# Sliding-window attention into a two-layer MLP on one core: weight slices in other places, and DMA transposes from step 13 on

## The chip, the core and the metric

One core of a Trainium2 chip runs the kernel. TensorE multiplies matrices into PSUM, VectorE, ScalarE and GpSimd work elementwise, and DMA queues move data between device memory and SBUF. Each engine takes its instructions in its own fixed order and waits at semaphores. SyncE computes nothing here: its queue issues nearly all DMAs, one after the other, and an entry that waits holds back all entries behind it. The metric is the device time of one execution in microseconds (us).

## The reference

Attention over 8 batches and 8 heads with 512 local and 32 global tokens each (head size 64), then a MLP over the 4608 rows of 512:

```python
def _attn_ref(q_l, k_l, v_l, q_g, k_g, v_g):
    ...
    s_g = scale * q_g @ k_all.T                  # 32 global queries see all 544 keys
    out_g = sm(s_g) @ v_all
    s_ll = where(abs(i - j) <= 32, scale * q_l @ k_l.T, -1e9)
    s_l = concatenate([scale * q_l @ k_g.T, s_ll])
    out_l = sm(s_l) @ concatenate([v_g, v_l])    # 512 local queries: window and globals
    return concatenate([out_g, out_l])

def _moe_ref(x, w_in, w_out):                    # 512 -> 2048 -> 512
    h = x @ w_in
    return (h / (1 + exp(-h))) @ w_out
```

All inputs and the output are float32.

## The kernel before

**Attention** is cut into 128 steps. A step k is one batch, one chunk of 128 queries and one pair of heads. Its parts are functions: `st_load` brings q and k into a `raw` tile (L314 for k < 28, L316 after), `st_split` makes two halves of them (k >= 28 only), `st_scores` does the scores s (L352 for k < 28) and the softmax (L359 to L368) into one of the `probs` tiles, `st_turn` transposes the probabilities on TensorE (L396) and copies them to a `pt` tile (L398), and `st_out` multiplies `pt` with v (o, L429) into the rows xh and xl of the MLP. From step KF = 24 on the transposes are done otherwise: `st_halves` has GpSimd sort the probabilities into two planes of 16 bit halves (L378, two copies a step), `st_away` writes these to device memory (L383), and `st_back` reads them back by a DMA transpose into `pt` (L387). Four `pt` tiles rotate. The 32 global queries go through `g_load` (L233), `g_scores` (L260), `g_soft` and `g_turn` (t and gt), four g steps a batch.

**The MLP** runs in 12 blocks n of 3 tiles (the last two: 2) of 128 rows. A block goes through the 16 slices f of the hidden layer: `first_layer` does 12 matmuls h (L584), then tanh on ScalarE (L590), gh and gl on VectorE and ScalarE (L591 to L594), and `second_layer` adds nine matmuls per f to the output banks (L606 to L608), one f later. The steps of the next block's tiles are spread over the matmuls of a block. Steps 0 to 13 come ahead of block 0, steps 14 to 25 lie in it.

**The weights** arrive as 64 bit words, only once, in slices i = 2f + half (half 0 the input weights of f, half 1 the output weights). `fetch_weights` issues the load of a slice (L195, names raw_w{i}), `join_weights` makes float32 of it on ScalarE (L213) and VectorE (L215, L216), and `split_weights` makes w_hi (ScalarE, L225) and w_lo (VectorE, L226), which h of that f waits for. In block 0, ahead of the first layer of f, the program joins up to f + 2 (LOOK) and fetches up to f + 5 (FETCH); the split of f + 1 follows.

**Places.** A slice's raw words lie in places that others use as well: half 0 of f in the place of w_hi of f; half 1 of f < 8 in that of w_hi of f + 8; half 1 of f >= 8 in the two `qk` tiles for odd f, and in the single tiles of the tags `o` and `halves` for even f. With two `qk` tiles, slice 27 (f = 13) has the place of slice 23 (f = 11). `raw_tile` gives a step's or a g step's load one of two `raws` tiles; for the first 28 steps and three batches of g loads it also uses the places 14 and 15 of later w_hi, four in rotation, until slices are fetched into these.

The order on TensorE and SyncE is written by the program: every part of a step has a due time, and the entries are emitted in the order of these times (`put`, `advance`, `fill`). On VectorE, ScalarE and GpSimd a scheduler sets the order.

Of the kernel before, what the change touches and what calls it, by code (L numbers as in the profile page):

```python
# [12 lines left out]
I32 = mybir.dt.int32  # L13
# [8 lines left out]
P = 128  # L22
# [5 lines left out]
SKV = SG + SL  # L28
DM, DFF = H * D, 2048
NCC, NF = DM // P, DFF // P  # L30
QW, KW, VW = 2 * P, 2 * W, 4 * D
# [5 lines left out]


SIZES = (3,) * 10 + (2, 2)
BUFS = dict(qk=2, raw=2, p=2, halves=1, pt=4)  # L40
ND = 28
KF = 24
GF = 3
KP = 12
WARM = 288
WARMS = (14, 8, 3)
SINGLE = 12
SCRATCH = 8
FETCH, LOOK = 6, 3
FIRSTW = {4: 2, 5: 2, 6: 1, 7: 1, 8: 1, 9: 1, 10: 1, 11: 1}  # L50
JOINS, SPLITS = (9.0, 9.6, 10.2, 10.8, 11.4, 12.0), (12.1, 12.7)

# [5 lines left out]
DMAT = dict(load=-1.65, halves=0.7, away=1.05, turn=1.3, back=1.65, out=2.7)  # L58
# [9 lines left out]
def attention_moe_kernel(ctx: ExitStack, tc: tile.TileContext, qk0_in, qk_in, v_in, gqk, wts, out):  # L68
    nc = tc.nc

    const = ctx.enter_context(tc.tile_pool(name="const", bufs=1))
    raws = ctx.enter_context(tc.tile_pool(name="raws", bufs=BUFS["raw"]))
    work = ctx.enter_context(tc.tile_pool(name="work", bufs=1))
# [23 lines left out]
    hold = tc.keep_in_program_order  # L97
    zeros = two.tile([P, WARM], BF16, tag="gl", bufs=1, name="zeros")
    nc.vector.memset(zeros, 0.0)

    def warm(bank, n):
        for _ in range(n):
            nc.tensor.matmul(bank[:, 512 - WARM :], zeros[:, :P], zeros, start=True, stop=True)

# [5 lines left out]

    probs = [const.tile([P, 2, 2 * P], F32, name=f"probs{i}") for i in range(BUFS["p"])]
    more = scratch(6, F32, "probs_")
# [9 lines left out]
    for kind in range(3):  # L122
# [7 lines left out]
        if kind == 0:  # L130
            hold(nc.gpsimd.memset(m[:, :HALO], NEG))
            pads()
            id32 = work.tile([P, P], F32R, tag="qk", bufs=BUFS["qk"], name="id32").bitcast(F32)
            make_identity(nc, id32)
# [9 lines left out]

    pts = [const.tile([P, 2, 2, P + SG], F32, name=f"pt{i}") for i in range(BUFS["pt"])]
    for t in pts:
# [5 lines left out]
    def probs_tile(k):  # L152
        i = k % (len(probs) if k < KP else BUFS["p"])
        held_by[i] = k
        return probs[i]
# [8 lines left out]
    def raw_tile(name, whole=False):  # L164
        i = next(homes) if whole else 0
        if whole and i == NPR:
            return scratch(13, F32, name)
        i = (i - (i > NPR)) % 4
        if i % 2 and 14 + i // 2 not in taken:
            return scratch(14 + i // 2, F32, name)  # L170
        return raws.tile([P, QW + KW], F32, tag="raw", name=name)

    def qk_tiles(name):
        return (work.tile([P, QW + KW], F32R, tag="qk", bufs=BUFS["qk"], name=f"qk{name}"),
                work.tile([P, SKV], F32R, tag="klo", bufs=BUFS["qk"], name=f"klo{name}"))

    w_32, w_hi, w_lo, w_raw, w_next = [], [], [], [], [0, 0]

    def fetch_weights():
        i = w_next[0]
        w_next[0] += 1
        f, half = divmod(i, 2)
        if half and f >= SCRATCH:
            homes_ = [work.tile([P, QW + KW], I32, tag="qk", bufs=BUFS["qk"], name=f"raw_w{i}_{q}")[:, :DM] if f % 2
                      else work.tile([P, DM], I32, tag="halves" if q else "o", bufs=1, name=f"raw_w{i}_{q}")
                      for q in range(2)]
        else:
            taken.add(f + SCRATCH * half)  # L190
            homes_ = [scratch(f + SCRATCH * half, I32, f"raw_w{i}")]
        n = DM // len(homes_)
        w_raw.append([(raw, q * n, n) for q, raw in enumerate(homes_)])
        for raw, c0, n in w_raw[i]:
            hold(nc.sync.dma_start(out=raw, in_=wts[f, :, DM * half + c0 : DM * half + c0 + n].bitcast(I32)))  # L195

    def join_weights():
        i = w_next[1]
        w_next[1] += 1
        while w_next[0] <= i:  # L200
            fetch_weights()
        f = i // 2
        if f + 1 == NF:
            w_32.append(work.tile([P, SKV], F32, tag="klo", bufs=BUFS["qk"], name=f"w{i}")[:, :DM])
        elif i % 2 == 0:
            w = const.tile([P, 2 * DM], F32, tag=f"ws{f + 1}", name=f"w{f}")
            w_32.extend((w[:, :DM], w[:, DM:]))
        for raw, c0, n in w_raw[i]:
            join_words(w_32[i][:, c0 : c0 + n], raw)
# [19 lines left out]
    state = {}  # L229

    def g_load(b, p):
        raw = raw_tile(f"raw_g{b}_{p}", b < GF)
        hold(nc.sync.dma_start(out=raw[:, :GW], in_=gqk[b, p]))  # L233
        state["graw", p] = raw

# [73 lines left out]
    tiles = {}  # L309

    def st_load(k, b, c, pr):
        raw = raw_tile(f"raw{k}", k < ND)
        if k < ND:
            hold(nc.sync.dma_start(out=raw[:, : QW + W], in_=qk0_in[k]))  # L314
        else:
            hold(nc.sync.dma_start(out=raw, in_=qk_in[k - ND]))  # L316
        tiles["raw", k] = raw
# [72 lines left out]
    def st_turn(k, b, c, pr):  # L390
        if k < KF:
            t = attbank("t", f"t{k}")
# [89 lines left out]
    at = 0.0  # L482

    def put(when, fn, *a):
        stream.append((when, fn, a))

    AHEAD = NPR
    for k, (t, b, c, pr) in enumerate(steps):
        a = (k, b, c, pr)
        j = k % NST  # L490
        due = dict(DUE)
        if k >= KF:
            due.update(DMAT if k >= ND else {part: DMAT[part] for part in DMAT if part != "load"})
            due.update({} if pr else DMAT0)
        if k < AHEAD:
            due.update({part: FIRST[part][k] - k for part in ("load", "vload", "turn", "out")})
        elif pr == 0:
            due["vload"] = VLOADS[min(k // NPR, 3)]
        if k == AHEAD:
            for h in range(NPR):  # L500
                put(FIRST["gload"][h], g_load, 0, h)
                put(FIRST["gscores"][h], g_scores, 0, h)
            for hh in range(2):
                put(FIRST["gsoft"][hh], g_soft, 0, hh)
                put(FIRST["gturn"][hh], g_turn, 0, hh)
            put(FIRST["late"], g_late)
            at = FIRST["then"]
            for when in JOINS:
                put(at + when - NPR, join_weights)
            for f, when in enumerate(SPLITS):  # L510
                put(at + when - NPR, split_weights, f)
        if j == 0 and b:
            for hh in range(2):
                put(at + (TURN if b > 1 else TURN1)[hh], g_turn, b, hh)
        for i in range(FIRSTW.get(k, 0)):
            put(at + 0.01, fetch_weights)
        put(at + due["load"], st_load, *a)
        put(at + due["split"], st_split, *a)
        put(at, st_scores, *a)
        if "vload" in due:  # L520
            put(at + due["vload"], st_vload, *a)
        if k >= KF:
            put(at + due["halves"], st_halves, *a)
            put(at + due["away"], st_away, *a)
        put(at + due["turn"], st_turn, *a)
        if k >= KF:
            put(at + due["back"], st_back, *a)
        if k < SINGLE or pr == NPR - 1:
            n = 1 if k < SINGLE else NPR
            put(at + due["out"], st_out, k - n + 1, n, b, c, t)  # L530
            marks[t] = at + due["out"]
        if j == NST - 1 and b % 4 == 3:
            put(marks[t] + 0.001, g_tile, t + 1)
            marks[t + 1] = marks[t] + 0.001
        if b + 1 < B:
            for h in [h for h in range(NPR) if int((HEADS if b else HEADS0)[0] + h * (HEADS if b else HEADS0)[1]) == j]:
                for part, fn in (("load", g_load), ("split", g_split), ("scores", g_scores)):
                    put(at + HEAD[part], fn, b + 1, h)
                if h % 2:
                    put(at + HEAD["soft"], g_soft, b + 1, h // 2)  # L540
                at += HEAD["slot"]
        at += 1.0
# [80 lines left out]
    for n in range(len(SIZES)):  # L623
        for f in range(NF):
            if n == 0:
                while w_next[1] < 2 * min(NF, f + LOOK):
                    join_weights()
                while w_next[0] < 2 * min(NF, f + FETCH):
                    fetch_weights()
            elif f == 0:  # L630
                advance(ends[n])
                now[:] = n, 0
            while len(w_hi) < NF and len(w_hi) <= NF * n + f + 1:
                split_weights(len(w_hi))
            g = first_layer(n, f)
            fill(SIZES[n])
            if pend is not None:
                second_layer(*pend)
            pend = (n, f, *g)
# [70 lines left out]
```

## Time and profile before

| | |
|---|---|
| median of 3 timed runs | 1020.4 us (1020.23 to 1022.18) |
| the profiled execution's own time | 1019.24 us |
| its span, first to last instruction | 1017.4 us |
| TensorE busy | 973.6 us, 96% |
| VectorE, ScalarE, GpSimd busy | 619.3, 580.6, 180.6 us |
| mean granted TensorE clock | 0.985 of full speed |
| DMA | 151.03 MB, 148 GB/s on the mean |

A busy share is a mean over stages with different limits: the attention ahead of block 0 (0 to 47 us), block 0, in which the weights come in, and eleven blocks without weights. The views used below are the busy times by windows, the waits (who waited for whom, in total), the chain of work that ended last, the timeline of one engine or queue, and the groups of instructions by line. In the last, a row reads: line, engine, operation, out<-in, shapes, count | busy us, mean ns of one | idle time before it and what ended it.

### The profile page before, as it was taken

How to read it: one execution, taken by the hardware profiler on the slowest of the kernel's cores; microseconds unless marked ns; L12 is line 12 of the kernel's file. 1: busy time of each engine (PE TensorE's matmuls, PEld its weight loads, DVE VectorE, ACT ScalarE, POOL GpSimd, SP SyncE). 2: the span in 40 equal slices, each digit the busy share in tenths (PEclk: the TensorE clock that was granted, in tenths of full speed). 3: DMA queues.
4: the chain of work that ended last, by engine and by line, in shares of the span. 5: the costliest groups of instructions: out<-in, count | busy, mean ns of one | idle time of the engine just before them, and what ended most of it. 6: DMA issues, size and time to landing. Idle time of an engine off the chain costs nothing.

```text
span 1017.4 us, 17554 instructions
## 1 busy us (share of the span) xinstructions
PE 973.6 (96%) x5838; PEld 861.2 (85%) x5838; DVE 619.3 (61%) x1894; ACT 580.6 (57%) x1491; POOL 180.6 (18%) x389
## 2 busy tenths in 40 slices
PE   8987769999999999999999999999999999999998
PEld 6666658879899898998989989999999999889896
DVE  5866466556577566765566666675677665543322
ACT  7965546556665655654466665665566655444332
POOL 2000000222222221312222212222213221211000
PEclk9998889999999999999999999999999999999999
DMA  9852352656766566454376566565667466433000
GB/s 289 285 178 90 123 153 57 188 148 170 185 173 173 140 191 182 133 167 114 84 204 172 151 185 179 158 172 142 176 172 201 125 168 180 101 99 87 1 22 21
DMA packets 175626, 151.03 MB, mean 148 GB/s; under 512 B 115888, under 2 KB 135856, under 8 KB 175536
## 3 DMA queue, kind: packets, MB, share of 16 engines
q1 hardware_dynamic: 171312, 142.31, 50.3%
q10 hardware_dynamic: 4224, 7.60, 2.2%
q8 instruction: 46, 0.75, 0.3%
q14 instruction: 44, 0.36, 0.1%
HBM read 86.44 MB, written 36.18 MB: 121 GB/s over the span
## 4 chain that ended last, share of the span: by engine, by line
PE 78%; DMA 10%; DVE 6%; ACT 3%; issue 1%; SPq 1%; POOL 0%; ACTq 0%; DVEq 0%; POOLq 0%
PE h L584 31%; PE out L606 11%; PE out L608 11%; PE out L607 10%; DMA raw<-in_qk_dram 6%; PE o L429 6%; DMA away<-halves 2%; PE s L352 2%; PE s L354 2%; PE s L355 2%; DMA raw_g<-in_gqk_dram 1%; DVE w L216 1%; PE t L396 1%; PE gs L260 1%; ACT qk L336 1%
## 5 line engine op out<-in xcount | busy, mean ns | idle before, releaser
L584 PE MATMUL h<-xh,w_lo 128*128 128x384 f32 (+1 forms) x768 | 253.7, 330 | 3.6 <-DVE w_lo L226 3.5
L584 PE MATMUL h<-xh,w_hi 128*128 128x384 f32 (+1 forms) x768 | 254.3, 331 | 0.0
L584 PE MATMUL h<-xl,w_hi 128*128 128x384 f32 (+1 forms) x768 | 252.7, 329 | 0.0
L606 PE MATMUL out<-w_hi,gh 128*128 128x512 f32 x544 | 223.3, 410 | 1.8 <-ACT gh L593 1.6
L378 POOL COPY halves<-probs 128x512 uint16<-128x512 uint16 x208 | 136.2, 680 | 477.7 <-DVE probs L368 246.7
L608 PE MATMUL out<-w_hi,gl 128*128 128x512 f32 x544 | 216.3, 398 | 3.3 <-DVE gl L594 2.5
L607 PE MATMUL out<-w_lo,gh 128*128 128x512 f32 x544 | 215.4, 396 | 0.0
L590 ACT ACTIVATE t<-h 128x384 f32<-128x384 f32 (+1 forms) x192 | 90.4, 471 | 174.7 <-PE h L584 163.1
L591 DVE SCALAR_TENSOR_TENSOR t<-t,h 128x384 f32<-128x384 f32 (+1 forms) x192 | 101.7, 529 | 106.2 <-ACT t L590 105.0
L363 ACT ACTIVATE probs<-probs,st 128x224 f32<-128x224 f32 x244 | 115.7, 475 | 83.3 <-DVE st L359 82.7
L584 PEld LDWEIGHTS h<-xh,w_hi 128*128 128x128 f32 x768 | 145.7, 190 | 7.5 <-issue 0.6
L584 PEld LDWEIGHTS h<-xl,w_hi 128*128 128x128 f32 x768 | 145.7, 190 | 6.6
L584 PEld LDWEIGHTS h<-xh,w_lo 128*128 128x128 f32 x768 | 145.4, 189 | 4.9 <-DVE w_lo L226 4.9
L594 DVE TENSOR_TENSOR gl<-t,gh 128x384 fp32r<-128x384 f32 (+1 forms) x192 | 106.0, 552 | 64.3 <-PE out L608 47.4
L359 DVE CUSTOM_DVE_ANT_0 probs<-s,mask 128x224 f32<-128x224 f32 x244 | 85.5, 387 | 83.1 <-PE s L355 53.6
L608 PEld LDWEIGHTS out<-w_hi,gl 128*128 128x128 f32 x544 | 103.0, 189 | 31.4 <-DVE gl L594 8.2
L593 ACT CAST gh<-t 128x384 fp32r<-128x384 f32 (+1 forms) x192 | 94.5, 492 | 56.2 <-DVE t L591 55.7
L606 PEld LDWEIGHTS out<-w_hi,gh 128*128 128x128 f32 x544 | 103.7, 191 | 22.3 <-ACT gh L593 5.4
L607 PEld LDWEIGHTS out<-w_lo,gh 128*128 128x128 f32 x544 | 103.8, 191 | 13.0
L336 ACT CAST qk<-raw 128x704 fp32r<-128x704 f32 x100 | 77.6, 776 | 34.8 <-DMA raw<-in_qk_dram 27.6
L337 DVE TENSOR_TENSOR klo<-raw,qk 128x448 fp32r<-128x448 f32 x100 | 65.4, 654 | 42.5 <-ACT qk L336 41.1
L367 ACT ACTIVATE probs<-probs,st 128x224 f32<-128x224 f32 x122 | 58.7, 481 | 35.6 <-DVE st L366 33.5
(91 smaller groups left out, 1081.1 us busy)
## 6 DMA issues: line engine op xcount, KB each, us to landing
raw<-in_qk_dram SPq DMA_DIRECT2D x100, 352.0 KB, 3.3
away<-halves SPq DMA_DIRECT2D x104, 256.0 KB, 2.6
vraw<-in_v_dram SPq DMA_DIRECT2D x30, 512.0 KB, 4.8
raw_w<-in_wts_dram SPq DMA_DIRECT2D x24, 512.0 KB, 6.9
raw_g<-in_gqk_dram SPq DMA_DIRECT2D x32, 304.0 KB, 4.3
out_dram<-o ACTq DMA_DIRECT2D x28, 256.0 KB, 3.5
raw<-in_qk_dram SPq DMA_DIRECT2D x28, 240.0 KB, 4.7
raw_w<-in_wts_dram SPq DMA_DIRECT2D x16, 256.0 KB, 4.0
```

Of the source, the lines that this page charges most:

```text
L336: nc.scalar.copy(out=qk, in_=raw)
L359: nc.vector.tensor_tensor_reduce(out=p[:, u, :W], in0=ss[u], in1=mask_of[c], scale=-SCALE, scalar=3.0e38, op0=ALU.add, op1=ALU.min, accum_ ...
L363: nc.scalar.activation(p[:, u, :W], p[:, u, :W], AF.Exp, bias=st[:, u : u + 1], scale=-1.0, accum_out=st[:, 2 + u : 3 + u])
L378: nc.gpsimd.tensor_copy(out=halves[:, :, u], in_=p[:, 2 * P * u : 2 * P * (u + 1)].bitcast(U16).rearrange("p (j h) -> p h j", h=2))
L584: nc.tensor.matmul(h[:, :nt], wt, x[:, c, :nt], start=(i == 0), stop=(i == 3 * NCC - 1))
L590: nc.scalar.activation(t[:, :nt], h[:, :nt], AF.Tanh, scale=0.5)
L591: nc.vector.scalar_tensor_tensor(out=t[:, :nt], in0=t[:, :nt], scalar=1.0, in1=h[:, :nt], op0=ALU.add, op1=ALU.mult)
L593: nc.scalar.copy(out=gh[:, :nt], in_=t[:, :nt])
L594: nc.vector.tensor_tensor(out=gl[:, :nt], in0=t[:, :nt], in1=gh[:, :nt].bitcast(F32), op=ALU.subtract)
L606: nc.tensor.matmul(o, gh[:, sl], wh, start=(f == 0), stop=False)
L607: nc.tensor.matmul(o, gh[:, sl], wl, start=False, stop=False)
L608: nc.tensor.matmul(o, gl[:, sl], wh, start=False, stop=(f == NF - 1))
```

## The change

The second halves of slices from f = 8 on are fetched one f later than the first halves, and for even f into the two `klo` tiles, which no step uses before step 28. FETCH becomes 5. Steps from 9 on and g loads of batches 1 and 2 use only the two `raws` tiles. The probabilities are turned by GpSimd copies and DMA transposes from KF = 12 on (the 13th step), and the tag `halves` has two tiles. Loads of steps 12 to 27 take the earlier due time of `DMAT`.

```diff
-BUFS = dict(qk=2, raw=2, p=2, halves=1, pt=4)
+BUFS = dict(qk=2, raw=2, p=2, halves=2, pt=4)
-KF = 24
+KF = 12
+WHOLE = 9
-FETCH, LOOK = 6, 3
+FETCH, LOOK = 5, 3
...
-    def fetch_weights():
-        i = w_next[0]
-        w_next[0] += 1
-        f, half = divmod(i, 2)
+    def fetch_weights(f, half):
+        i = 2 * f + half
         if half and f >= SCRATCH:
-            homes_ = [work.tile([P, QW + KW], I32, tag="qk", ...)[:, :DM] if f % 2
-                      else work.tile([P, DM], I32, tag="halves" if q else "o", bufs=1, ...)
-                      for q in range(2)]
+            tag, n = ("qk", QW + KW) if f % 2 else ("klo", SKV)
+            homes_ = [work.tile([P, n], I32, tag=tag, bufs=BUFS["qk"], ...)[:, :DM] for q in range(2)]
...
-        raw = raw_tile(f"raw_g{b}_{p}", b < GF)
+        raw = raw_tile(f"raw_g{b}_{p}", b == 0)
...
-        raw = raw_tile(f"raw{k}", k < ND)
+        raw = raw_tile(f"raw{k}", k < WHOLE)
...
         if k >= KF:
-            due.update(DMAT if k >= ND else {part: DMAT[part] for part in DMAT if part != "load"})
+            due.update(DMAT)
...
             if n == 0:
-                while w_next[1] < 2 * min(NF, f + LOOK):
+                while w_next[0] < 2 * min(NF, f + LOOK):
                     join_weights()
-                while w_next[0] < 2 * min(NF, f + FETCH):
-                    fetch_weights()
+                for g, half in ((f + FETCH, 0), (f + FETCH - (f + FETCH > SCRATCH), 1)):
+                    if g < NF and 2 * g + half not in w_raw:
+                        fetch_weights(g, half)
```

SyncE's queue in block 0, at f = 7 and 8, before. A row is line, operation, out<-in, shape and the kinds of semaphores it waits for; raw20 is the load of step 20, raw_w27_0 the first part of slice 27:

```order
L195 DMA raw_w24_1226<-in_wts_dram 128x1024 [waits DMAHW0_49]
L195 DMA raw_w25_0_1228<-in_wts_dram 128x512 [waits DMAHW1_49,DVE_49]
L195 DMA raw_w25_1_1229<-in_wts_dram 128x512 [waits DMAHW2_49,DVE_49]
L314 DMA raw20_1271<-in_qk0_dram 128x480 [waits DMAHW3_49,PE_49]
L195 DMA raw_w26_1298<-in_wts_dram 128x1024 [waits DMAHW4_49]
L195 DMA raw_w27_0_1300<-in_wts_dram 128x512 [waits DMAHW5_49,DVE_49,Activation_49]
L195 DMA raw_w27_1_1301<-in_wts_dram 128x512 [waits DMAHW6_49,DVE_49,Activation_49]
L314 DMA raw21_1346<-in_qk0_dram 128x480 [waits DMAHW7_49,PE_49]
```

The same place of the queue now (the changed file's lines are 2 to 4 lower):

```order
L310 DMA raw20_1218<-in_qk0_dram 128x480 [waits PE_49]
L193 DMA raw_w24_1230<-in_wts_dram 128x1024 [waits DMAHW2_49]
L193 DMA raw_w23_0_1232<-in_wts_dram 128x512 [waits DMAHW3_49,DVE_49]
L193 DMA raw_w23_1_1233<-in_wts_dram 128x512 [waits DMAHW4_49,DVE_49]
L383 DMA_TRANSPOSE pt1_130<-away17_1209 128x4x256 [waits DMAHW5_49,DMAHW0_49,Pool_49]
L379 DMA away18_1284<-halves18_1263 128x1024 [waits DMAHW6_49,Pool_49]
L193 DMA raw_w26_1299<-in_wts_dram 128x1024 [waits DMAHW7_49]
L193 DMA raw_w25_0_1301<-in_wts_dram 128x512 [waits DVE_49]
L193 DMA raw_w25_1_1302<-in_wts_dram 128x512 [waits DMAHW1_49,DVE_49,Activation_49]
L310 DMA raw21_1332<-in_qk0_dram 128x480 [waits DMAHW2_49,PE_49]
```

The load of step 21 stood behind slice 27, whose place is free when slice 23 is joined, which the program does at f = 9; it now stands behind slice 25, whose place is free when slice 21 is joined, at f = 8. One transpose and one write of halves of earlier steps have come in between.

TensorE in block 0, between the first layers of f = 12 and f = 13, before (out of f = 11; t21 the transposes of step 21, s23 the scores of step 23):

```order
L584 MATMUL h0_12_1593<-xh_0_244,w_lo12_1525 128x384
L396 MATMUL t21_1613<-ident_108,probs1_86 128x128 x4
L606 MATMUL out0_0_799<-w_hi11_1434,gh0_11_1544 128x512
L607 MATMUL out0_0_799<-w_lo11_1435,gh0_11_1544 128x512
L608 MATMUL out0_0_799<-w_hi11_1434,gl0_11_1545 128x512
L352 MATMUL s23_1623<-raw23_1550 128x224 x2
L606 MATMUL out0_1_800<-w_hi11_1434,gh0_11_1544 128x512
```

And now:

```order
L580 MATMUL h0_12_1605<-xl_0_245,w_hi12_1529 128x384
L580 MATMUL h0_12_1605<-xh_0_244,w_lo12_1530 128x384
L348 MATMUL s23_1625<-raw23_1475 128x224 [waits DMAHW6_49,PE_49]
L348 MATMUL s23_1625<-raw23_1475 128x224
L602 MATMUL out0_0_804<-w_hi11_1449,gh0_11_1549 128x512 [waits Activation_49]
L603 MATMUL out0_0_804<-w_lo11_1450,gh0_11_1549 128x512
L604 MATMUL out0_0_804<-w_hi11_1449,gl0_11_1550 128x512 [waits DVE_49]
```

The transposes are gone, and the scores of a step stand three matmuls earlier than before.

More of the change, by code (lines that the diff above doesn't have):

```diff
@@ L175, in qk_tiles @@
                 work.tile([P, SKV], F32R, tag="klo", bufs=BUFS["qk"], name=f"klo{name}"))
-    w_32, w_hi, w_lo, w_raw, w_next = [], [], [], [], [0, 0]
-    def fetch_weights():
-        i = w_next[0]
-        w_next[0] += 1
-        f, half = divmod(i, 2)
+    w_32, w_hi, w_lo, w_raw, w_next = [], [], [], {}, [0]
+    def fetch_weights(f, half):
+        i = 2 * f + half
         if half and f >= SCRATCH:
-            homes_ = [work.tile([P, QW + KW], I32, tag="qk", bufs=BUFS["qk"], name=f"raw_w{i}_{q}")[:, :DM] if f % 2
-                      else work.tile([P, DM], I32, tag="halves" if q else "o", bufs=1, name=f"raw_w{i}_{q}")
-                      for q in range(2)]
+            tag, n = ("qk", QW + KW) if f % 2 else ("klo", SKV)
+            homes_ = [work.tile([P, n], I32, tag=tag, bufs=BUFS["qk"], name=f"raw_w{i}_{q}")[:, :DM] for q in range(2)]
         else:
@@ L192, in fetch_weights @@
         n = DM // len(homes_)
-        w_raw.append([(raw, q * n, n) for q, raw in enumerate(homes_)])
+        w_raw[i] = [(raw, q * n, n) for q, raw in enumerate(homes_)]
         for raw, c0, n in w_raw[i]:
@@ L197, in join_weights @@
     def join_weights():
-        i = w_next[1]
-        w_next[1] += 1
-        while w_next[0] <= i:
-            fetch_weights()
+        i = w_next[0]
+        w_next[0] += 1
         f = i // 2
@@ L515, in attention_moe_kernel @@
         for i in range(FIRSTW.get(k, 0)):
-            put(at + 0.01, fetch_weights)
+            put(at + 0.01, fetch_weights, *divmod(sum(FIRSTW.get(j, 0) for j in range(k)) + i, 2))
         put(at + due["load"], st_load, *a)
@@ L625, in attention_moe_kernel @@
             if n == 0:
-                while w_next[1] < 2 * min(NF, f + LOOK):
+                while w_next[0] < 2 * min(NF, f + LOOK):
                     join_weights()
-                while w_next[0] < 2 * min(NF, f + FETCH):
-                    fetch_weights()
+                for g, half in ((f + FETCH, 0), (f + FETCH - (f + FETCH > SCRATCH), 1)):
+                    if g < NF and 2 * g + half not in w_raw:
+                        fetch_weights(g, half)
             elif f == 0:
```

## The prediction

> **What bounds the kernel now.** I read the stages first, then the waits of the stage that stands out, then the chain of work inside it. In the view by windows (columns: stretch and its length, busy time of PE, PEld, DVE, ACT and POOL with instruction counts, granted TensorE clock, DMA share, GB/s) the stretches are the attention ahead of block 0, block 0 (from its first first-layer matmul at 47.1 us to that of block 1 at 178.7), and blocks 1, 2 and 3:
>
> ```profile
> 0.00:47.10 47.10, 41.72 (x297) 30.00 (x297) 31.48 (x139) 39.99 (x121) 7.75 (x41) 1.00 0.88 294
> 47.10:178.70 131.60, 104.65 (x544) 89.25 (x543) 83.06 (x242) 76.96 (x194) 5.19 (x14) 0.90 0.39 123
> 178.70:262.50 83.80, 81.65 (x466) 70.82 (x466) 50.57 (x156) 48.43 (x126) 18.76 (x36) 1.00 0.61 167
> 262.50:346.00 83.50, 82.53 (x505) 74.28 (x502) 57.50 (x178) 52.70 (x135) 19.68 (x41) 1.00 0.63 172
> 346.00:430.00 84.00, 82.15 (x499) 73.58 (x499) 55.59 (x171) 49.62 (x126) 19.74 (x41) 1.00 0.64 171
> ```
>
> Blocks 1 to 3 take 84 us each with TensorE busy for 82, so TensorE bounds them and little can be had there. Block 0 runs the same two layers over three tiles and takes 131.6 us, 47.6 more. TensorE is idle for 27 us of it (131.6 less 104.65), and it is busy for 22.5 us longer than in block 3, part of which is the clock, 0.90 on the mean. The waits between 50 and 175 us (us in total, times, longest), of the engines and then of SP's queue, say who holds it:
>
> ```profile
> PE s L352 <- DMA raw<-in_qk_dram: 22.6, 6, 6.2
> DVE probs L359 <- PE s L352: 21.7, 7, 5.7
> PE h L584 <- DVE w_lo L226: 3.5, 3, 2.6
> ...
> SPq L195 <- DVE raw_w L215: 47.3, 4, 20.9
> SPq L195 <- DVE w L216: 15.2, 8, 7.4
> SPq L195 <- PE gs L260: 12.6, 1, 12.6
> ```
>
> TensorE waits for the q and k of a step, and VectorE for the scores. The loads are not slow: SP's queue stands still for 75 us in front of weight slices (L195) whose place is taken. The chain in order of time (start, length) and SP's timeline show one round:
>
> ```profile
> 107.96 0.44 DVE w L216
> 108.41 0.33 SPq L195
> 108.83 4.81 DMA raw<-in_qk_dram
> 113.78 1.85 PE s L352 x4
> ...
> 162.46 0.44 PE t L396 x4
> 162.90 0.23 PE out L606
> 178.82 2.11 PE h L584 x12
> 186.36 0.76 PE s L352 x4
> ...
> 96.75 11.98 SPq L195 DMA_DIRECT2D raw_w<-in_wts_dram  x3
> ```
>
> VectorE joins a slice, its place comes free, the next slice is issued after 12 us of standing, and only then the load behind it, which lands 4.8 us later into a TensorE that has run dry. It is a ring: the join stands in VectorE's order behind the softmax of the step whose load stands in SP's order behind the slice. The scores after such a gap take 1.85 us where they take 0.76 at the full clock, so a gap costs more than its length.
>
> **The change, part by part.** The sum is made against the profiled execution, 1019.24 us (span 1017.4; the median of the three timed runs, 1020.4, is 1.2 higher).
>
> *Slices where their place is free.* The second halves from slice 17 on are fetched one f later, and each now waits only for a join that stands ahead of its fetch in the program, where before it waited for one that stood behind it. The tightest load is that of step 21: it stands behind slice 25, which waits for the join of slice 21, and its scores come after the split of f = 9 (two of L226, 1.3 us), a first layer (2.11) and a second (nine of 0.23, 2.1), 5.5 us after that join, against two issues of 0.4 and a landing of 4.81. The others have a layer or two more. I cost the waits of s at nothing after the change; what hides them is that lead, and if it is gone the 22.6 us come back. So up to 47.6 us less the new limits below. The 12.6 us for the place of a g load (L260) go as well, since steps from 9 on and the g loads of batches 1 and 2 no longer live in places of weights.
>
> *Two raw places instead of four from step 9 on.* This adds a wait: a load is issued only when the scores two loads back are done. Rows of SP's and TensorE's timeline, and the landing of the loads up to 60 us:
>
> ```profile
> 38.07 0.33 SPq L314 DMA_DIRECT2D raw<-in_qk_dram  x1
> ...
> 37.12 0.92 PE L352 MATMUL s<-raw 128*128 128x224 f32 x4
> 41.83 1.03 PE L352 MATMUL s<-raw 128*128 128x224 f32 x4
> 46.39 1.02 PE L352 MATMUL s<-raw 128*128 128x224 f32 x4
> ...
> DMA to landing us min/median/max: 2.6/5.2/8.4
> ```
>
> The scores at 37.12, 41.83 and 46.39 are those of steps 11, 12 and 13. Before, the load of step 13 went out at 38.07, 8.3 us early. After, that of step 12 can go only at 38.07, when the scores of step 11 end, and at the median lands at 43.3, 1.5 us after TensorE wanted it; that of step 13 then goes at 44.3 and lands at 49.5, 3.1 late. At the fastest landing, 2.6, nothing is late; at the slowest, 8.4, 46.5 and then 55.9, 9.5 late. I take 2.5, close under the median, because fewer slices travel beside these loads. This delays the start of block 0.
>
> *Turning by DMA from step 13 on (k = 12).* Removed are 12 times four transposes on TensorE, 0.44 us a step, 5.3 us, and 12 copies on ScalarE:
>
> ```profile
> L398 ACT COPY pt<-t 128x512 f32<-128x512 f32 x12 | 7.0, 582 | 9.3 <-PE t L396 9.1
> ...
> L226 DVE TENSOR_TENSOR w_lo<-w,w_hi 128x512 fp32r<-128x512 f32 x29 | 18.8, 688 | 0.0
> L216 DVE SCALAR_TENSOR_TENSOR w<-w,raw_w 128x512 uint32<-128x512 uint32 x18 | 12.4, 691 | 4.0 <-ACT w L213 3.7
> L594 DVE TENSOR_TENSOR gl<-t,gh 128x384 fp32r<-128x384 f32 x15 | 8.3, 557 | 10.5 <-ACT gh L593 6.3 <-PE out L608 4.1
> ...
> L378 POOL COPY halves<-probs 128x512 uint16<-128x512 uint16 x25 | 16.4, 682 | 52.1 <-DVE probs L368 24.3 <-DMA away<-halves 16.1 <-ACT probs L367 11.6
> L594 DVE TENSOR_TENSOR gl<-t,gh 128x384 fp32r<-128x384 f32 x16 | 9.5, 592 | 2.1 <-PE out L608 1.2 <-ACT gh L593 0.6
> ```
>
> The first four rows are block 0, the last two block 3. ScalarE falls from 77 to 70 us. Added are 24 copies on GpSimd, 24 x 0.682 = 16.4 us on an engine busy for 5.2. The price beside it shows in L594: 557 ns in block 0, where GpSimd rests, 592 in block 3, where it copies. Those 6.3% on the 39.5 us of the three VectorE rows of block 0 are 2.5 us; the ends are 0, if the weights' operations are spared, and 16.4, if each copy stops VectorE for its whole length. I take 2.5, from the nearest row. The Trainium skill, page "SBUF — State Buffer", section "Who interferes with whom", speaks against this part: a VectorE instruction with two SBUF inputs contends with a GpSimd instruction that reads SBUF, and the loser stands still. By it the sum could be worse by as much as the end above; the 35 ns say that a copy seldom meets one.
>
> On SP each step gets two more entries, and these wait (rows for blocks 1 to 11, 104 turned steps):
>
> ```profile
> SPq L387 <- DMA away<-halves: 190.4, 81, 4.9
> SPq L383 <- POOL halves L378: 141.2, 61, 8.3
> SPq L387 <- PE o L429: 107.1, 22, 9.7
> ...
> L387 SPq DMA_TRANSPOSE pt<-away x104: 1226/1227/2431, 177.2 to 932.6; - x104
> ...
> q1 hardware_dynamic: 18288, 13.44, 61.2%
> raw<-in_qk_dram SPq DMA_DIRECT2D x12, 352.0 KB, 3.8
> vraw<-in_v_dram SPq DMA_DIRECT2D x3, 512.0 KB, 4.5
> raw_g<-in_gqk_dram SPq DMA_DIRECT2D x4, 304.0 KB, 3.5
> ...
> q1 hardware_dynamic: 7839, 16.07, 38.5%
> ```
>
> Behind a waiting away or transpose stand the next step's load and slices, and TensorE's o waits for the transpose. In blocks 1 to 11 that costs TensorE nothing (2 us idle of 84), with loads two steps ahead; I cost it at nothing in block 0 too. One spot is tighter: the transpose of step 19 stands behind slice 27, which waits for the join of slice 23, and o of steps 16 to 19 comes some 5 us after that join; at the 4.81 us that a load takes this may stall TensorE for 0 to 3 us, inside the margin below.
>
> DMA time: block 3 spends 61.2% of 84 us, 51.4, on this queue. Its loads are 12 x 0.360 + 3 x 0.524 + 4 x 0.311 = 7.15 MB, at block 0's 16.07 MB in 50.7 us (317 GB/s) 22.6 us; the other 28.8 us are 12 aways and 12 transposes. Block 0 would need 50.7 + 28.8 = 79.5 us.
>
> *Two places for halves* let GpSimd copy a step while the last one leaves; 16.1 us of its waiting goes, on an engine that holds up nobody now. I cost it at nothing in blocks 1 to 11, where TensorE idles 1 to 2 us a block.
>
> *What is late next.* Block 0 then has TensorE work of 84 us (like blocks 1 to 3), VectorE 83.1 + 2.5 = 85.6, DMA 79.5, ScalarE 70. VectorE is the fullest, and its weight work lies in the first fourteen sixteenths. In-order engines this close don't run at 100%: ahead of block 0 the two fullest reached 0.85 (ScalarE, 39.99 of 47.1) and 0.88 (DMA). At 0.95 the block takes 90 us, at 0.85 101; 0.885, just above those rows since the loads have more lead, gives 97. Sum: 1019.24 - 131.6 + 97 + 2.5 = 987.1.
>
> **The rivals.**
> 1. *TensorE sets the pace.* VectorE's joins run in TensorE's shadow as its work in blocks 1 to 3 does, and block 0 takes 84 to 89 us: 972 to 979 with up to 2.5 for the start. Against it: TensorE already waited for w_lo (3.5 us) with VectorE only 63% busy.
> 2. *GpSimd's copies or VectorE's own waits hold VectorE.* With 16.4 us of full stops its load is 99.5 us, at 0.885 112 us: 1002. The page named above is this rule. The 557 to 592 speaks against it; that block 0's VectorE work is nearly all of the two-input kind speaks for it. Half of it gives 103 us and 993.
> 3. *The slices still hold the loads.* A second half's place still waits for a join, now one of the same f. If VectorE comes to that join an f later than SP, the ring stays closed, and half to nine tenths of the 34.6 us that the forecast saves in block 0 stay away: 114 to 128 us, 1004 to 1018. That is also how the change would fail to do what it says. For it speaks the 5.5 us of step 21, against it that the other steps have more.
> 4. *Slower: SP's queue becomes the ring.* Per step the away and transpose waits are (190.4 + 141.2 + 107.1) / 104 = 4.2 us, the transpose's issue 1.2, the slice waits of before (47.3 + 15.2) / 12 = 5.2, other issues 1.4: 12 us if none overlaps, 144 for twelve steps, 1034. It decides at 131.6 / 12 = 11 us a step. Against it: most of this standing is SP being early, as TensorE's 82 of 84 us in block 3 beside the same waits show.
>
> **How the numbers follow.** The forecast (block 0 in 90 to 103 us, 980 to 993) 0.56; rival 1 0.15; rival 2 0.19; rival 3 0.06; rival 4 0.03; no change 0.01. The range 976 to 1002 takes in the upper half of rival 1 and all of rival 2. About 0.2%, 2 us, is what a measurement of this kernel tells from no change; so faster 0.96, same 0.01, slower 0.03.
>
> **What the profile of the changed kernel would show.** The wait of s for raw under 4 us and SP's wait at slices without a load's lateness behind it; block 0's granted clock above 0.97; w_lo as TensorE's first releaser in block 0; DVE busy there 84 to 88 us, at 85% or more of the stretch; no t group after step 11; block 0 starting at 48 to 51 us; blocks 1 to 11 within 1 us of before. I am wrong if s still waits for raw, if block 0 takes under 88 or over 103 us, or if L226 and L216 grow by over 15% beside the copies.

## The result, and the profile after

The changed kernel takes 995.99 us (median of 4 runs, 992.51 to 997.79) against 1020.32 us before (4 runs, 1017.85 to 1022.18): a ratio of 0.976, 95% interval [0.972, 0.980]. That is faster, inside the forecast's range, and 9 us above its point: it lies in the range that rival 2 gave (993 to 1002), not in the forecast's own (980 to 993). The profiled execution took 994.48 us (span 992.6).

The stages after, by windows (columns as before: stretch, length, busy time of PE, PEld, DVE, ACT, POOL, granted clock, DMA share, GB/s): the attention ahead of block 0, block 0 (47.5 to 150.1, again from its first h matmul to that of block 1), and all that follows:

```profile
0.00:47.50 47.50, 41.97 (x297) 30.45 (x297) 31.50 (x139) 40.05 (x121) 8.65 (x42) 1.00 0.79 259
...
47.50:150.10 102.60, 92.19 (x500) 75.42 (x499) 88.87 (x245) 71.34 (x186) 22.90 (x39) 1.00 0.85 235
...
150.10:992.60 842.50, 828.06 (x4998) 741.01 (x4996) 507.24 (x1511) 463.01 (x1174) 169.26 (x332) 1.00 0.53 143
```

The same stretch before, from block 1 to the end:

```profile
178.70:1017.40 838.70, 827.25 (x5002) 741.97 (x5000) 504.75 (x1514) 463.69 (x1177) 167.62 (x334) 1.00 0.53 144
```

Block 0 fell from 131.6 to 102.6 us, its start moved by 0.4, and blocks 1 to 11 grew by 3.8: 1019.24 + 0.4 - 29.0 + 3.8 = 994.4. The clock in block 0 went from 0.90 to 1.00 (0.98 in the repeat below), and VectorE is busy for 88.87 of 102.6 us, 87%. The waits in block 0 (us in total, times, longest), of PE and of SP's queue:

```profile
PE h L580 <- DVE w_lo L222: 6.7, 6, 2.1
PE o L425 <- POOL pt L401: 2.3, 2, 1.3
PE s L348 <- DMA raw<-in_qk_dram: 0.5, 1, 0.5
...
SPq L383 <- DMA away<-halves: 18.6, 6, 4.7
SPq L193 <- DVE raw_w L211: 18.6, 5, 5.4
SPq L193 <- DVE w L212: 5.7, 8, 3.0
```

The scores no longer wait for raw: 0.5 us in place of 22.6. SP still stands in front of slices (24.3 us in place of 62.5), but 5.4 at most and with no late load behind. First of TensorE's waits is now w_lo, VectorE's product. The larger groups of VectorE in block 0 whose duration changed most, and GpSimd's copies (busy us, mean ns):

```profile
L222 DVE TENSOR_TENSOR w_lo<-w,w_hi 128x512 fp32r<-128x512 f32 x29 | 19.2, 702 | 0.3 <-ACT w_hi L221 0.3
L212 DVE SCALAR_TENSOR_TENSOR w<-w,raw_w 128x512 uint32<-128x512 uint32 x18 | 16.1, 894 | 3.2 <-ACT w L209 2.4
L590 DVE TENSOR_TENSOR gl<-t,gh 128x384 fp32r<-128x384 f32 x15 | 9.1, 609 | 1.7 <-ACT gh L589 1.1 <-PE out L604 0.6
...
L374 POOL COPY halves<-probs 128x512 uint16<-128x512 uint16 x27 | 18.3, 702 | 74.2 <-DVE probs L364 46.4 <-issue 15.3 <-DMA raw_w<-in_wts_dram 11.8
```

The wide join L212 (L216 before) went from 691 to 894 ns, 29%; w_lo only from 688 to 702, gl from 557 to 609, and the shift ahead of the wide join (L211, 128x512) from 422 to 446. The timeline of GpSimd and of VectorE around two of the joins (start, length) shows why this one:

```profile
100.25 1.24 POOL L374 COPY halves<-probs 128x512 uint16<-128x512 uint16 x2 [5.91 <-DVE probs L364]
106.17 1.25 POOL L374 COPY halves<-probs 128x512 uint16<-128x512 uint16 x2 [4.68 <-DVE probs L364]
...
101.03 1.00 DVE L212 SCALAR_TENSOR_TENSOR w<-w,raw_w 128x512 uint32<-128x512 uint32 x1
...
106.86 1.10 DVE L212 SCALAR_TENSOR_TENSOR w<-w,raw_w 128x512 uint32<-128x512 uint32 x1 [0.47 <-ACT w L209]
```

GpSimd's copies come in pairs and start when VectorE has finished the softmax (L364). Behind that stand in VectorE's order the shift of a wide slice (L211, 0.42 us) and soon its join. So ten of the 13 pairs in block 0 meet a wide join. The narrow joins that follow find GpSimd at rest and take 423 ns, as before.

### The profile page after: what moved, and what is told of

Read it like the earlier page. It is cut to its first block, busy times and chain, and to the rows that moved or that the text cites. A ratio compares the mean times of both kernels' runs of the same rounds, so it can differ in the third digit from the quotient of the medians.

```text
span 992.6 us, 17536 instructions
## 1 busy us (share of the span) xinstructions
PE 962.2 (97%) x5790; PEld 846.9 (85%) x5790; DVE 627.6 (63%) x1894; ACT 574.4 (58%) x1479; POOL 200.8 (20%) x413
## 4 chain that ended last, share of the span: by engine, by line
PE 72%; DMA 9%; DVE 4%; ACT 3%; issue 2%; SPq 1%; POOL 0%; ACTq 0%; DVEq 0%; POOLq 0%
PE h L580 29%; PE out L602 10%; PE out L604 10%; PE out L603 10%; PE o L425 6%; DMA raw<-in_qk_dram 5%; DMA raw_g<-in_gqk_dram 2%; PE s L350 2%; PE s L351 2%; DMA away<-halves 1%; ACT qk L332 1%; DVE w L212 1%; DVE gl L590 1%; PE gt L296 1%; DVE w_lo L222 0%
## 5 line engine op out<-in xcount | busy, mean ns | idle before, releaser
L374 POOL COPY halves<-probs 128x512 uint16<-128x512 uint16 x232 | 154.1, 686 | 529.3 <-issue 319.7
L602 PEld LDWEIGHTS out<-w_hi,gh 128*128 128x128 f32 x544 | 102.6, 189 | 28.1 <-ACT gh L589 11.6
```

Of the source, the lines that this page charges most:

```text
L374: nc.gpsimd.tensor_copy(out=halves[:, :, u], in_=p[:, 2 * P * u : 2 * P * (u + 1)].bitcast(U16).rearrange("p (j h) -> p h j", h=2))
L602: nc.tensor.matmul(o, gh[:, sl], wh, start=(f == 0), stop=False)
```

## The experiments

Unless it says otherwise, each is the changed kernel with the edit shown. "Rest" is the span less the start of block 0 and less block 0. Of the profiled executions, in us:

| kernel | median | ratio to before | start | block 0 | rest |
|---|---|---|---|---|---|
| before | 1020.3 | 1 | 47.1 | 131.6 | 838.7 |
| changed kernel | 996.0 | 0.976 [0.972, 0.980] | 47.5 | 102.6 | 842.5 |
| changed kernel again | 994.0 | 0.975 [0.972, 0.978] | 48.3 | 103.0 | 842.4 |
| 1 turn on TensorE | 987.7 | 0.968 [0.966, 0.971] | 47.4 | 99.7 | 838.1 |
| 1 once more | 989.4 | 0.969 [0.966, 0.972] | 47.4 | 99.9 | 840.2 |
| 2 idle copies | 991.7 | 0.974 [0.971, 0.977] | 48.1 | 102.9 | 839.3 |
| 3 copies on ScalarE | 997.1 | 0.977 [0.973, 0.980] | 47.4 | 104.8 | 843.8 |
| 4 no low words | 985.1 | 0.966 [0.963, 0.969] | 47.5 | 91.9 | 844.6 |
| 5 old fetch | 1020.3 | 1.001 [0.999, 1.003] | 47.1 | 126.6 | 842.6 |
| 6 four raw places | 999.6 | 0.981 [0.979, 0.984] | 47.3 | 107.9 | 843.3 |
| 7 fetch only | 998.2 | 0.980 [0.977, 0.983] | 48.1 | 105.3 | 844.2 |
| 8 one halves | 993.7 | 0.973 [0.970, 0.977] | 48.3 | 102.8 | 841.5 |
| 9 as 1, one halves | 991.5 | 0.972 [0.969, 0.976] | 47.8 | 99.8 | 848.3 |
| 10 half of the turn | 996.4 | 0.977 [0.974, 0.979] | 47.1 | 106.4 | 839.9 |

The changed kernel was run again beside experiments 1, 3 and 4, on one chip:

> The changed kernel itself, unaltered, for comparison on this chip. Both theories: ratio to before 0.972 to 0.980; block 0 between 100 and 105 us; blocks 1 to 11 together 839 to 844 us if their 3.9 us over before is the change's, 837 to 840 if it was the scatter of one execution.

Measured: 993.95 us (993.37 to 995.82), block 0 103.0, rest 842.4: what blocks 1 to 11 lose came a second time. TensorE's mean clock in block 0 was 0.98 here and 1.00 there, and the block is only 0.4 us longer.

### 1. The turn back on TensorE

```diff
-KF = 12
+KF = 24
```

> Undoes the DMA turn of steps 12 to 23 alone (KF back to 24); slices, two raw places and two halves places stay as changed. Theory A (VectorE sets the pace of block 0, and GpSimd's copies lengthen its instructions): the wide join on VectorE (L212, 128x512) falls from 894 to about 690 ns, VectorE's load in block 0 from 88.9 to 83 to 84 us, TensorE's work rises by 5.3 us to 97.5, and block 0 takes 98 to 102 us: 0 to 5 us faster than the changed kernel, so the turn was worth nothing or a little less than nothing. Rival (the turn by DMA gains what TensorE saves): block 0 takes 107 to 109 us, 5 us slower than the changed kernel.

Measured: 987.73 us (986.50 to 988.62), 6.2 less than the changed kernel beside it. Block 0 in the same views:

```profile
47.35:147.07 99.72, 95.20 (x544) 81.90 (x542) 82.57 (x242) 75.72 (x194) 5.91 (x14) 0.98 0.54 175
...
L222 DVE TENSOR_TENSOR w_lo<-w,w_hi 128x512 fp32r<-128x512 f32 x29 | 18.9, 691 | 0.0
L212 DVE SCALAR_TENSOR_TENSOR w<-w,raw_w 128x512 uint32<-128x512 uint32 x18 | 12.4, 692 | 2.4 <-ACT w L209 1.6
...
L590 DVE TENSOR_TENSOR gl<-t,gh 128x384 fp32r<-128x384 f32 x15 | 8.3, 554 | 3.7 <-ACT gh L589 3.6
```

The join is back at 692 ns, VectorE's busy time at 82.6, and the block is 2.9 us shorter although TensorE does 48 transposes more. So in block 0 the DMA turn costs more than it saves. The edit also puts the loads of steps 12 to 23 back to their old due time; experiment 2 leaves them there and has a block 0 of 102.9 all the same. This variant was run again on another chip:

> The best variant so far once more: the changed kernel with steps 12 to 23 turned by TensorE, as before the change. If it is a better version than the changed kernel, its ratio is again 0.967 to 0.970, with block 0 at 99 to 100.5 us and blocks 1 to 11 at 838 to 839.5. Rival (the first run was a lucky one): 0.972 or more, blocks 1 to 11 at 841 us or more.

Measured: 989.42 us (987.06 to 990.83), ratio 0.969, block 0 99.9, rest 840.2. It is a better version than the changed kernel, again; the rest came out between the two expectations.

### 2. The copies alone, for nobody

On top of 1, GpSimd makes the copies of steps 12 to 23 without a DMA behind them:

```diff
+        elif k >= 12:
+            put(at + DMAT["halves"], st_idle, *a)
```

> As the changed kernel, but steps 12 to 23 are turned by TensorE (the variant that took 987.7 us), and GpSimd makes the 24 copies of halves for these steps all the same, for nobody: they leave no result and no DMA reads them. Theory A (the copies themselves lengthen VectorE's two-input instructions): the wide join goes from 692 to 850 to 900 ns, the gl row from 554 to 590 to 610, VectorE's busy time in block 0 from 82.6 to 87 to 89 us, block 0 from 99.7 to 102 to 104, in all 990 to 993 us. Rival (the way out to DRAM and back, not the copy, is what the turn costs): the rows of VectorE stay or block 0 stays within 1 us of 99.7, 987 to 988.5 us.

Measured: 991.68 us, block 0 102.9. The groups and the stretch:

```profile
48.12:151.02 102.90, 96.21 (x544) 81.69 (x543) 87.04 (x242) 75.86 (x194) 21.20 (x37) 0.98 0.53 169
...
L212 DVE SCALAR_TENSOR_TENSOR w<-w,raw_w 128x512 uint32<-128x512 uint32 x18 | 15.0, 834 | 1.8 <-ACT w L209 1.2
...
L599 DVE TENSOR_TENSOR gl<-t,gh 128x384 fp32r<-128x384 f32 x15 | 9.1, 608 | 2.9 <-ACT gh L598 2.9
```

The copies by themselves lengthen the join to 834 ns and block 0 by 3.0 to 3.2 us (102.9 against 99.7 and 99.9), as much as the whole turn does, with a DMA share of 0.53 in place of 0.85. TensorE still does its 48 transposes here, so the way through device memory and what it saves on TensorE come to nothing together; what the turn costs in block 0 is GpSimd's copies beside VectorE. In the rest, 839.3, nothing is lost here.

### 3. The copies on ScalarE

```diff
-            nc.gpsimd.tensor_copy(out=halves[:, :, u], in_=...)
+            src = ...
+            if k < 24:
+                nc.scalar.copy(out=halves[:, :, u], in_=src)
+            else:
+                nc.gpsimd.tensor_copy(out=halves[:, :, u], in_=src)
```

> The changed kernel with the 24 copies into halves of steps 12 to 23 on ScalarE instead of GpSimd; all DMAs and TensorE's work stay. Theory A: L212 wide back to about 690 ns, VectorE's load in block 0 to 83 to 84 us, block 0 to 97 to 100 us, 3 to 5 us faster than the changed kernel, unless ScalarE, at 71 + 12 to 16 us, gets in the way. Rival B (the DMA queue, 85% busy in block 0, sets the pace): L212 shorter, but block 0 within 1.5 us of 102.6.

Measured: 997.13 us, block 0 104.8:

```profile
47.43:152.24 104.81, 93.89 (x499) 76.42 (x498) 84.62 (x245) 82.69 (x209) 7.22 (x16) 0.98 0.86 230
...
L212 DVE SCALAR_TENSOR_TENSOR w<-w,raw_w 128x512 uint32<-128x512 uint32 x18 | 12.5, 692 | 2.9 <-ACT w L209 1.6
...
PE o L428 <- issue: 3.7, 1, 3.7
```

The join is at 692 ns again, which once more puts its growth on GpSimd, but the time does not follow: ScalarE is at 82.7 us, nearly as full as VectorE, and a new gap of 3.7 us stands before an o. That this o waited for a turn that left late is likely, not shown. Here, freeing VectorE by filling ScalarE to nearly the same level gained nothing. VectorE's busy time alone doesn't give the block's: 4.25 us less of it, and the block is 2.2 us longer.

### 4. A smaller join

The low words of the weights are left out of the join, and with them the three lowest bits of each weight's mantissa.

```diff
-        hold(nc.vector.tensor_scalar(out=low, in0=low, scalar1=29, ..., op0=ALU.logical_shift_right))
-        hold(nc.vector.scalar_tensor_tensor(out=wi, in0=wi, scalar=3, in1=low, ...))
+        hold(nc.vector.tensor_scalar(out=wi, in0=wi, scalar1=3, scalar2=None, op0=ALU.logical_shift_left))
```

> The changed kernel with the low words of the weights left out of the join: no shift of them, and the join on VectorE becomes a shift of the high word alone (the three lowest mantissa bits are lost). DMAs, TensorE, ScalarE and GpSimd keep their work; VectorE loses 12.6 us of L211 and some of L212 in block 0. Theory A: block 0 falls towards TensorE's own 92 us, to 93 to 96, 7 to 10 us faster than the changed kernel. Rival B (the DMA queue at 85%): block 0 within 2 us of 102.6.

Measured: 985.10 us, block 0:

```profile
47.47:139.38 91.91, 89.25 (x500) 76.12 (x499) 70.73 (x211) 70.78 (x185) 22.09 (x39) 1.00 0.94 263
```

With 18.1 us less on VectorE block 0 is 10.7 us shorter, at a DMA share of 0.94. So VectorE set its pace, and DMA did not. Now TensorE does: 89.25 of 91.9 us. Block 0's own TensorE work is thus some 89 us, where blocks 1 to 3, from which the prediction took its 84 us, are busy for 82. A part of the difference is that the scores of a step below 28 take 0.76 us (the row in the prediction), while the four matmuls of a later step take 0.44 (from 375.09 to 375.53 us in the kernel before): for some 12.5 steps that is 4 of the 7 us, an estimate.

### 5. The old moment of the fetch

```diff
-                for g, half in ((f + FETCH, 0), (f + FETCH - (f + FETCH > SCRATCH), 1)):
-                    if g < NF and 2 * g + half not in w_raw:
+                for g, half in itertools.product(range(min(NF, f + 6)), range(2)):
+                    if 2 * g + half not in w_raw:
```

> The changed kernel with one thing undone: at each f of block 0 both halves of every slice up to f + 5 are fetched, as before, so a second half's place again waits for a join that stands behind it in the program. Theory A (the moment of the fetch is what opened the ring): the scores wait for raw 15 to 25 us again, block 0 takes 120 to 130 us in place of 102.6, 1012 to 1022 us. Rival (the other places and the DMA turn carry the gain): under 3 us above the changed kernel, at most 997.

Measured: 1020.26 us, no different from before. Block 0:

```profile
47.12:173.72 126.60, 98.34 (x500) 81.59 (x499) 89.58 (x245) 71.36 (x186) 22.96 (x39) 0.89 0.69 191
...
PE s L348 <- DMA raw<-in_qk_dram: 12.2, 3, 7.0
PE o L425 <- DMA pt<-away: 10.7, 2, 6.0
...
SPq L193 <- DVE raw_w L211: 49.4, 6, 11.6
```

The ring is closed again: SP stands for 49.4 us before slices, and behind them come late both loads (12.2; the expectation had 15 to 25) and transposes (10.7), since both sit in the same queue. With the other parts of the change in place and the moment of the fetch undone, nothing is won. The converse, the new moment with the even slices still in the places `o` and `halves`, was not run, so the `klo` places may be needed too.

### 6. The places of the loads undone

```diff
-WHOLE = 9
+WHOLE = 28
-        raw = raw_tile(f"raw_g{b}_{p}", b == 0)
+        raw = raw_tile(f"raw_g{b}_{p}", b < GF)
```

> The changed kernel with the places of the loads undone: steps 0 to 27 and the g loads of batches 0 to 2 use places of weights again (four raw places in place of two). Theory A (the fetch opened the ring, and the two places from step 9 on cost the start nothing): block 0 still starts at 47 to 48 us; SP waits some 12 us for the g load's place behind the scores of g again, which makes loads late by 3 to 8 us in block 0: 997 to 1003. Rival 1 (the places don't matter): within 2 us of the changed kernel's 994 to 996. Rival 2 (two places delay the start, hidden in other gains): the start comes 1 to 2.5 us earlier than 47.5 and the time falls to 991 to 993.

Measured: 999.64 us, block 0 107.9, start 47.3:

```profile
PE s L348 <- DMA raw<-in_qk_dram: 6.4, 3, 5.4
...
SPq L193 <- PE gs L256: 5.8, 1, 5.8
SPq L193 <- DMA raw_g<-in_gqk_dram: 5.0, 1, 5.0
```

Slices wait 10.8 us in all for the place of a g load, and the longest wait of scores for a load is 5.4 us. The two raw places carry 5.3 us of the gain, and the start doesn't notice them.

### 7. The fetch alone

On top of 6: KF = 24 and one place for halves, so that of the change only the moments and places of the slices are left.

> Of the whole change only the slices: when they are fetched and which places the second halves take. The turn of steps 12 to 23 stays on TensorE, the loads keep four raw places and the g loads theirs, and halves has one place. Theory A (the fetch carries nearly all of the gain): the scores wait for raw under 4 us, block 0 takes 99 to 104 us, 985 to 992 us in all. Rival (the loads' places are needed for it): SP waits 10 us or more for the g load's place, the scores 5 us or more for raw, block 0 takes 108 us or more, 996 to 1008.

Measured: 998.18 us, block 0 105.3:

```profile
PE s L348 <- DMA raw<-in_qk_dram: 3.9, 2, 3.0
...
SPq L193 <- PE gs L256: 12.6, 1, 12.6
```

Between the two expectations: the fetch alone takes 26.3 us off block 0. The standing for the g load's place remains, and block 0 is 5.5 us longer than in experiment 9, which has the two raw places and is otherwise the same.

### 8 and 9. One place for halves, with and without the turn

```diff
-BUFS = dict(qk=2, raw=2, p=2, halves=2, pt=4)
+BUFS = dict(qk=2, raw=2, p=2, halves=1, pt=4)
```

> The changed kernel with one place for halves in place of two. Theory A (the second place frees GpSimd, which holds up nobody): the whole time stays within 2 us of the changed kernel's 994 to 996, block 0 within 1.5 us of 102.6, and blocks 1 to 11 stay at 842 to 843.5 us. Rival (the second place shifts GpSimd's copies, and these the loads of blocks 1 to 11): blocks 1 to 11 return to 838 to 840, 989 to 992 us in all.

Measured: 993.67 us, block 0 102.8, rest 841.5: no difference. Yet the copies now meet other instructions of VectorE:

```profile
L222 DVE TENSOR_TENSOR w_lo<-w,w_hi 128x512 fp32r<-128x512 f32 x29 | 20.1, 731 | 0.3 <-ACT w_hi L221 0.3
L212 DVE SCALAR_TENSOR_TENSOR w<-w,raw_w 128x512 uint32<-128x512 uint32 x18 | 13.3, 740 | 3.3 <-ACT w L209 2.2
```

> The variant with steps 12 to 23 turned by TensorE (987.7 us, blocks 1 to 11 in 838.1), with one place for halves. Theory A (the 4 us that blocks 1 to 11 lose come with the turn in block 0): blocks 1 to 11 at 838 to 839.5, block 0 at 99 to 101, 986.5 to 989.5 us. Rival (any shift of the loads' moments costs or saves such an amount, the turn is not the cause): blocks 1 to 11 at 841 to 845, 990 to 994 us.

Measured: 991.50 us (989.25 to 997.70), block 0 99.8. The profiled execution, the longest of the six, has a rest of 848.3, outside both expectations. The interval overlaps that of experiment 1. So a kernel that turns no step before 24 by DMA can lose time in the rest too.

### 10. Half of the turn

```diff
-KF = 12
+KF = 18
```

> The changed kernel with the DMA turn from step 18 on in place of step 12: half of the turned steps of block 0 go back to TensorE. Theory A (each of GpSimd's copies lengthens VectorE's two-input work, and the copies run beside most of the weights' joins): block 0 halfway, 100 to 102 us, in all 989 to 993. Rival (the cost sits in the early steps, when VectorE is behind by most): block 0 at 99 to 100 us as without the turn, 986 to 989.

Measured: 996.39 us, block 0 106.4. Both expectations missed: half of the turn makes block 0 longer than either all of it or none. Its waits:

```profile
PE h L580 <- DVE w_lo L222: 6.0, 5, 2.1
PE s L348 <- ACT pt L394: 1.9, 1, 1.9
PE s L348 <- DMA raw<-in_qk_dram: 1.2, 1, 1.2
```

It has nearly the waits for w_lo of the changed kernel (6.7) and more than the waits of s that experiment 1 has (0.6 and 0.5). VectorE is busy for 86.81 us, less than in the changed kernel. What makes the block longer was not followed further, so the account below does not cover it.

## Why the prediction was right or wrong

**The sum.** For the profiled execution 987.1 were forecast and 994.48 measured. The terms missed by 2.1 us downward (the start) and by 5.6 and 3.8 upward (block 0, and blocks 1 to 11). The time lies in the stated range, but above the forecast's own 980 to 993. Of the signs named, three did not come: VectorE busy for 84 to 88 us in block 0 (88.87), a start at 48 to 51 us (47.5), and blocks 1 to 11 within 1 us of before.

**The ring: right.** The forecast costed the waits of s for raw at nothing; they measure 0.5 us. Experiment 5 brings the ring and the time back. In block 0 the fetch is worth 26.3 us (7) or 24.0 (5), the raw places 5.3 to 5.5 (6; 7 against 9), the second halves place 0 (8, 9), and the turn -2.9 (1): -26.3 - 5.5 + 2.9 = -28.9 of the -29.0 measured. These runs form a chain from before to after, each one edit from the next, so the sum has to come out; what backs it up are experiments 5 and 6, which price the fetch and the places from the other end. Rivals 3 and 4 fell with it.

**The start: 2.5 us forecast, 0.4 measured, and not from the two places.** With four places it started at 47.1, 47.3 and 48.1, with two at 47.1 to 48.3. The loads of steps 12 and 13 did go out late as forecast, at 38.43 and 43.26 us, each when the scores two loads back were done, but both landed in 2.5 us. The step that failed took the median landing over the first 60 us, 5.2. TensorE waits for no load ahead of block 0. The landings between 28 and 60 us of the changed kernel, then that of raw before:

```profile
raw_w<-in_wts_dram SPq DMA_DIRECT2D x8, 512.0 KB, 5.7
raw<-in_qk_dram SPq DMA_DIRECT2D x6, 240.0 KB, 2.7
...
raw<-in_qk_dram SPq DMA_DIRECT2D x3, 240.0 KB, 4.6
```

**GpSimd's copies: mis-sized, 2.5 us forecast, 5.8 measured.** VectorE's load in block 0 is 88.87, not 85.6 (83.06 before). The 6.3% were read from gl (L594) in block 3, where GpSimd copies without a join near. In block 0 the copies start at the softmax's end, shortly ahead of a wide join, which grows by 29%: 3.7 of the 5.8 us (0.8 are gl, 0.4 each w_lo and the shift, and 0.4 one L364 more). Growth of over 15% had been named as a sign of being wrong for L226 and L216; it came for L216 alone. Experiment 2 shows that the copies alone do it. The Trainium skill, page "SBUF — State Buffer", section "Who interferes with whom", says that a VectorE instruction with two SBUF inputs contends with a GpSimd instruction that reads SBUF and that the loser stands still. The rows agree: the copies that began at 106.17 ended at 107.42, the join that began at 106.86 ended at 107.96, 0.54 after them, and alone it takes 0.69. In the whole of block 0 each of the ten joins that meet a pair of copies ends 0.54 to 0.56 us after that pair, and the other eight take 0.68 or 0.69. The upper end, 16.4, did not come: these ten joins run beside copies for 5.2 of the copies' 18.3 us.

**Block 0: 97 forecast, 102.6 measured.** At the forecast's 0.885 the measured load gives 100.4; the rest is the share, 0.866. Of the 5.6 us, 3.4 are the load and 2.2 the share. VectorE as the engine that sets the pace was right (4), but a load divided by one share is too simple: the share is 0.81 in experiments 3 and 10 and 0.83 in 1, so a lower load there did not always give a shorter block. TensorE's 84 us was a second wrong step: it needs 89, so rival 1's 84 to 89 us could hardly have been reached even with VectorE out of the way. Rival 2 is what happened, and its "half of it", 103 us and 993, came close partly by luck: that half is a load of 91.3 us at 0.885, measured were 88.87 at 0.866, and the 3.8 us that blocks 1 to 11 lost more than offset the 2.1 us by which the start came sooner.

**DMA.** 79.5 us were forecast, 84.7% of 102.6 = 86.9 measured; experiment 4 shows that it did not bind.

```profile
q1 hardware_dynamic: 22868, 24.03, 84.7%
```

**Blocks 1 to 11: nothing forecast, 3.8 us measured, and only partly explained.** Most of the loss shows in the wait of out for gh, here from block 1 to the end, of the changed kernel, of before and of experiment 1:

```profile
PE out L602 <- ACT gh L589: 6.0, 9, 1.5
```

```profile
PE out L606 <- ACT gh L593: 0.9, 2, 0.6
```

```profile
PE out L602 <- ACT gh L589: 1.7, 1, 1.7
```

One such place is in block 8. SP's and ScalarE's timeline of the changed kernel, then SP's of experiment 1 at the same entries:

```profile
729.53 0.50 SPq L379 DMA_DIRECT2D away<-halves  x1
730.13 0.37 SPq L229 DMA_DIRECT2D raw_g<-in_gqk_dram  x1
735.88 1.23 SPq L383 DMA_TRANSPOSE pt<-away  x1
737.22 0.52 SPq L312 DMA_DIRECT2D raw<-in_qk_dram  x1
...
742.46 0.78 ACT L332 CAST qk<-raw 128x704 fp32r<-128x704 f32 x1 [2.49 <-DMA raw<-in_qk_dram]
```

```profile
724.80 0.49 SPq L379 DMA_DIRECT2D away<-halves  x1
725.39 0.37 SPq L229 DMA_DIRECT2D raw_g<-in_gqk_dram  x1
729.59 1.23 SPq L383 DMA_TRANSPOSE pt<-away  x1
730.93 0.52 SPq L312 DMA_DIRECT2D raw<-in_qk_dram  x1
```

From the issue of the away to that of the transpose it is 6.35 us in one and 4.79 in the other. The step's load stands behind the transpose, ScalarE waits 2.49 us for it, and gh behind ScalarE's cast comes late to TensorE. What makes the away slower there is open. The loss is not tied to the turn: experiment 7, without it, has a rest of 844.2, and experiment 9 848.3. It is not one loss either: in experiment 9 the wait for gh is 2.7 us, but TensorE is busy for 832.0 us in place of 827.8 in experiment 1. One program gave 838.1 and 840.2 in experiment 1 and its repeat. All 14 executions lie between 838.1 and 848.3, so a term of "nothing" for these 840 us deserved some 5 us of margin.

## What to carry to other kernels

Where one queue issues everything in order, find what its entries wait for, and place an entry that waits for a computation only after that computation in the program: here this step, with the places that go with it, was worth 24 to 26 of 29 us, and without it the rest of the change won nothing. Price contention between two engines at the instruction that stands next to the copy in the stage concerned, not at the mean of another stage. The engine that is fullest in its stage, here VectorE at 87%, is the one to relieve, but not onto one that becomes nearly as full (experiment 3). Work moved off another engine (48 transposes off TensorE) gained nothing there: leaving them on TensorE is the faster version, 0.968 of the time before.

## What was not expected of the hardware

A VectorE join of two 128x512 uint32 inputs takes 0.69 us alone and up to 1.10 us when it meets a pair of GpSimd copies, 1.25 us together. In the changed kernel it ends 0.54 to 0.56 us after the pair each time. Others lose time too: gl took 0.97 us in place of 0.55 when it began just after a pair had begun (at 78.31 and 84.42 us), and a wide shift (L211), which has one tile as input, 0.84 in place of 0.42 (at 59.28). The join's growth comes with no DMA behind the copies (experiment 2: 834 ns on the mean with copies that nobody reads), and moving the copies to ScalarE takes it back to 692 ns.
